# 48 matmul products of the last pair on plain 32-bit floats, half of them split into two column halves

## The chip, the cores and the metric

The kernel runs on one core of a Trainium2 chip. The metric is the device time of one execution in microseconds; smaller is better. The core has five engines that work side by side, each on its own queue of instructions: TensorE (PE, the matmul array of 128 by 128 cells; its weight loads are listed apart, as PEld), VectorE (DVE), ScalarE (ACT), GpSimd (POOL) and SyncE (SP), which here issues the transfers between the device's memory and the on-chip memory.

## The reference

Two parts follow each other. Windowed attention, with 8 sequences, 8 heads, 576 positions and 64 numbers a head; each position sees itself and the 63 before it:

```
scores = scale * matmul(q, k.T); scores = where(mask, scores, -1e9)
attn   = softmax(scores);        x = matmul(attn, v)        # 4608 tokens x 512
```

Then a gated feed-forward layer on the 4608 tokens, with 512 inputs, 1536 hidden numbers and 512 outputs:

```
gate = 1 / (1 + exp(-(x @ w_gate)))
val  = x @ w_val
out  = (gate * val) @ w_out
```

All of it is in 32-bit floats, and the comparison is a tight one, so a single matmul in a shorter number format does not do.

## The kernel before, in words

**Numbers.** The big products use the rounded float type of TensorE (F32R), in which one matmul is a single record. To keep the accuracy, each operand is cut into a high part and the rest (hi and lo), and a product is three matmuls: hi times hi, hi times lo of the moving side, and lo of the weights times hi. That is `three` (L583 to L587; all its matmuls have line 586 in the profile). The attention's matmuls (scores L220, transposes L301, outputs L331) are on plain floats (F32), unsplit. The scores use quarters of the array (64 rows by 64 columns), the outputs column halves (128 rows by 64 columns), and neighbouring calls lie on different parts.

**Tiles.** The 4608 tokens are 12 tiles of 384 tokens (`TT`). Tiles 0 and 1 go through the feed-forward layer in the plain way (L353 to L415). Tiles 2 to 11 go in five pairs s = 1 to 5 (`NS` is 6, so the last is `NS - 1`). For a pair the matrix product is done by a scheme of Strassen's kind: 7 products of half-sized blocks in place of 8, listed in `PRODUCTS` (L422) as weight block, input block and the one of three accumulators (`b` = 0, 1, 2) that it goes to. A later product adds to what stands in its accumulator.

**The up stage of a pair.** It runs over `NK` = 6 blocks k of the hidden dimension, in each over the 7 products n, and in each over m = 0, 1 (gate and value). One `product(s, k, n, m)` (L613) is two calls of `three`, for the two halves c of the 256 input rows: 6 matmuls. So each n has 12 matmuls, each k has 84, and the stage has 504. Every matmul has 128 by 128 weights and 384 moving columns, and its result goes to 384 of the 512 columns of an accumulator bank. After each product `combine` (L589) reads the accumulator on ACT or DVE, makes the sums of the scheme, the sigmoid (L371) and the product of gate and value (L629).

**The down stage of a pair.** `last_product` (L678) calls the same `three`, 252 matmuls. The last pair has the last up stage and the last down stage, with no attention work among them.

**Order.** Every piece of work is put in a list with a due time and a rank (`put`, L708), the list is sorted, and the pieces are emitted in that order; a planner then orders each engine's queue, but the matmuls keep the written order (`pe`, L85). The weights of product n and block k come from memory by `w_load` (L433), issued on SP's queue, into one of 7 buffers (`WB`), which a load can take when PE has used what was in it.

Of the kernel before, what the change touches and what calls it, by code (L numbers as in the profile page):

```python
# [9 lines left out]
F32 = mybir.dt.float32  # L10
# [8 lines left out]
P = 128  # L19
BLK = 64  # L20
TT = 384
# [5 lines left out]
def attn_ffn(ctx: ExitStack, tc: tile.TileContext, qT, kT, vN, w_gate, w_val, w_out, out, outT):  # L27
# [3 lines left out]
    nc = tc.nc  # L31
# [9 lines left out]
    NS = NT // 2  # L41
# [37 lines left out]
    def psum(s, i, nm):  # L79
        return ps_b.tile([P, DM], F32, name=nm, tag=f"b{s % 2}{i}")  # L80
# [4 lines left out]
    def pe(ins):  # L85
        return tc.keep_in_program_order(ins)
# [79 lines left out]
    xs, xf = {}, {}  # L166
    ld, vts, st, kk, sc_of, sums_of = {}, {}, {}, {}, {}, {}
# [200 lines left out]
    def gate_table(t, j, c):  # L368
        g = mp.tile([P, TT], F32, name=f"g_{t}_{j}", tag="g", bufs=4)
        with table_order():  # L370
            act = nc.scalar.activation(g, c, AF.Sigmoid)  # L371
        chain.append(act.ins)
        marks["gate"] = act.ins
        gates[(t, j)] = g
# [53 lines left out]
    wt, wot = {}, {}  # L428
# [114 lines left out]
    def rhs_of(eng, src, nm):  # L543


        b11, b12, b21, b22, t1 = src
        if nm == "T2" and not any(src is x for x in t2_made):
            eng.tensor_sub(out=b11, in0=b22, in1=t1)
        elif nm == "T4":
            eng.tensor_sub(out=b11, in0=b21, in1=b11)  # L550
        return {"B11": b11, "T2": b11, "T4": b11, "T1": t1, "T3": b12, "B21": b21, "B22": b22}[nm]

    t2_made = []
    GUARD = (8, 13)

    def h_early(s, k):
# [23 lines left out]
        x2, src = xs[(s, n, c)]  # L580
        nc.vector.tensor_sub(out=x2[:, 1, :], in0=src, in1=x2[:, 0, :].bitcast(F32))

    def three(ps, w2, q, x2, first, last, check=True):  # L583
        whi, wlo = (w2[:, e, q * P:(q + 1) * P] for e in range(2))
        for i, (l, r) in enumerate(((whi, x2[:, 0, :]), (whi, x2[:, 1, :]), (wlo, x2[:, 0, :]))):
            pe(nc.tensor.matmul(ps, l, r, start=first and i == 0, stop=last and i == 2,  # L586
                                skip_group_check=not check))  # L587

    def combine(st, n, nm, emit):  # L589


        ps = st[PRODUCTS[n][2]][:, :TT]

        def plus(a, tag, bufs):
            o = mp.tile([P, TT], F32, name=f"{tag}{n}_{nm}", tag=tag, bufs=bufs)
            marks["plus"] = nc.vector.tensor_add(out=o, in0=ps, in1=a).ins  # L596
            return o

        if n == 0:
            st["p1"] = mp.tile([P, TT], F32, name=f"p1_{nm}", tag="p1", bufs=2)  # L600
            nc.scalar.copy(st["p1"], ps)
        elif n == 1:
            st["u2"] = plus(st["p1"], "u", 2)
        elif n == 3:
            emit(1, 1, st[2][:, :TT], plus(st["p1"], "c", CB))
        elif n == 4:
            emit(0, 0, ps, None)
        elif n == 5:
            emit(1, 0, ps, st["p1"])
        elif n == 6:  # L610
            emit(0, 1, ps, st["u2"])

    def product(s, k, n, m):  # L613
        st, b = acc[m], PRODUCTS[n][2]
        if n < 3:
            st[b] = psum(1 + m, b, f"pr{b}_{m}_{s}_{k}")
        for c in range(2):
            three(st[b][:, :TT], wt[(s, k, m, n)], c, xs[(s, n, c)][0], n < 3 and c == 0, c == 1, n < 3)

        def emit(r, b, in0, in1):  # L620
            t, j = 2 * s + b, k + r * NK
            c = in0
            if in1 is not None:
                c = mp.tile([P, TT], F32, name=f"c{n}_{m}_{s}_{k}", tag="c", bufs=CB)
                nc.vector.tensor_add(out=c, in0=in0, in1=in1)  # L625
            if m == 0:
                gate_table(t, j, c)
            else:
                nc.vector.tensor_mul(out=hidden(s, k)[2 * r + b], in0=c, in1=gates.pop((t, j)))  # L629

        combine(st, n, f"{m}_{s}_{k}", emit)

    def hidden(s, k):

        if (s, k) not in ht:
            nm = f"{s}_{k}"

            def one(tag, bufs, i):
                return mp.tile([P, TT], F32, name=f"h{i}_{nm}", tag=tag, bufs=bufs)

            def two(pool, tag, bufs, i):
                h2 = pool.tile([P, 2, TT], F32, name=f"h{i}_{nm}", tag=tag, bufs=bufs)
                return [h2[:, 0, :], h2[:, 1, :]]

            if k < 2:
                h5 = wts.tile([P, 5, TT], F32, name=f"h_{nm}", tag=f"wp_{k}")
                t = [h5[:, i, :] for i in range(5)]
            elif k == 2:
                t = [one("hh", 3, i) for i in range(3)] + [one("hl", 3, i) for i in range(3, 5)]
            else:  # L650
                t = two(mp, "raw", RAW, 0) + two(mp, "raw", RAW, 1)
                if k == 3:
                    t.append(one("hl", 3, 2))
                else:
                    if k == 4:
                        ht[(s, "last")] = two(wts, f"wo_{WOB}", 1, 2)
                    t.append(ht[(s, "last")][k - 4])
            ht[(s, k)] = t
        return ht[(s, k)]
# [5 lines left out]
    def h_split(nm, i, src):  # L665
        i %= EXTRA + 2 * NPR
        h2 = xp.tile([P, 2, TT], F32R, name=f"h_{nm}", tag=f"e{i}" if i < EXTRA else f"x{i - EXTRA}")
        nc.scalar.copy(h2[:, 0, :], src)  # L668
        nc.vector.tensor_sub(out=h2[:, 1, :], in0=src, in1=h2[:, 0, :].bitcast(F32))  # L669
        return h2  # L670

    def h_part(s, n, k):
        i = n * NK + k
        with tc.issue_after(marks["plus"]) if GUARD[0] <= i < GUARD[1] else nullcontext():
            hs[(s, n, k)] = h_split(f"{n}_{s}_{k}", i, rhs_of(nc.vector, hidden(s, k), PRODUCTS[n][1]))


    def last_product(s, n, k, qs=(0, 1)):  # L678
        b = PRODUCTS[n][2]
        for q in qs:  # L680
            st = acc[q]
            if n < 3 and k == 0:
                st[b] = psum(1 + q, b, f"y{b}_{q}_{s}")
            three(st[b][:, :TT], wot[(s, n, k)], q, hs[(s, n, k)], n < 3 and k == 0, k == NK - 1, n < 3)
            if k == NK - 1:
                combine(st, n, f"y{q}_{s}", lambda r, bb, in0, in1, q=q: emit_out(s, n, q, r, bb, in0, in1))
# [90 lines left out]
    for i in range(KINDS * NF):  # L777
        j, m = divmod(i, KINDS)
# [39 lines left out]
    for s in range(1, NS):  # L818
# [15 lines left out]
        for k in range(NK):  # L834
            if s == 1:
                for m in range(2):
                    make = (-28 + 7 * m, -29 + 6 * m)[k] if k < 2 else -25 + 8 * m
                    put(now + make - 6, 7, sums_load, m, k)
                    put(now + make, 7, sums_make, m, k)
                    for i, at_cut in zip((0, 2), (-14 + 2 * m, -10 + 2 * m) if k == 0 else (-13 + 1.5 * m, -5 + 1.5 * m)):  # L840
                        put(now + at_cut, 7, sums_split, m, k, i)
                        put(now + at_cut + 4, 7, sums_store, m, k, i)
                for n, d in ((0, -23 if k == 0 else -14), (4, -12 if k == 0 else -2), (5, -9 if k == 0 else -1)):
                    put(now + d, 7.5, w_load, s, k, n)
            else:
                for n in range(NPR):
                    put(now - 22 + 2.1 * n, 7.5, w_load, s, k, n)
            for n in range(NPR):
                for m in range(2):
                    put(now, 9, product, s, k, n, m)  # L850
                    now += PRT
                    if m == 0:
                        attend(("u", NPR * k + n - 0.5))
                attend(("u", NPR * k + n))
            put(now + 0.5, 5, h_prep, s, k)
            if k < EXTRA:
                put(now + 3, 5.1, h_early, s, k)
# [23 lines left out]
        for i, tm in enumerate(at_down):  # L881
            if i < EXTRA + 2 * NPR:
                when = max(t0 - 14.5 + 2.1 * ((i - EXTRA) // 2 + 1), t0 - 5.2 if GUARD[0] <= i < GUARD[1] else t0 - 15, {5: t0 + 0.8, 11: t0 + 0.9, 17: t0 + 1}.get(i, t0 - 20))
            else:
# [19 lines left out]
    for tm, _, f, a in events:  # L904
        if f in (conv_a, conv_b, conv_c):
            with ExitStack() as behind:
# [4 lines left out]
                j, m = divmod(a[0], KINDS)  # L911
# [56 lines left out]
```

## Time and profile before

| | |
|---|---|
| median of 2 runs | 961.32 us (961.26 to 961.37) |
| the profiled execution's own time | 961.67 us |
| its span, first to last instruction | 959.9 us |
| mean granted TensorE clock | 0.998 |
| matmul records in all | 7164 |
| of them on line 586, up products | 2520 |
| of them on line 586, down products | 1260 |

The profile is of one execution. A row of a group reads: line, engine, operation, output tile <- input tiles, array rows and columns used, partitions by elements, type, count, then busy time and mean duration. Both float types of TensorE are shown as f32. Matmuls are pipelined, and a recorded duration holds the way through the array; the time from one start to the next says how many fit in a stretch. "Idle before" is what an engine waited just ahead of the group.

### The profile page before, as it was taken

Reading aid. Unit: us, or ns where it says so; the run is one execution under the profiler, and the core shown is the slowest. Engines: PE = TensorE matmul, PEld = TensorE weight load, DVE = VectorE, ACT = ScalarE, POOL = GpSimd, SP = SyncE. Lnnn points to the kernel's source line nnn. Section 1 sums busy time; section 2 is a strip of 40 time slices with the busy share of each in tenths; the row PEclk is TensorE's granted clock in tenths of the full one; section 3 lists DMA queues with packets and bytes.
Section 4 is the critical chain, followed back from the end, with each engine's and each line's share of the span. In section 5 each row is a group of like instructions: output and inputs, shape, how many; then the busy total and the mean of one; then the engine's idle time right before and its main releaser. Section 6 shows DMA issues by size and latency. Waiting matters only on the chain.

```text
span 959.9 us, 20420 instructions
## 1 busy us (share of the span) xinstructions
PE 941.3 (98%) x7164; PEld 898.0 (94%) x7164; DVE 714.3 (74%) x1919; ACT 602.7 (63%) x1487; POOL 147.5 (15%) x232
## 2 busy tenths in 40 slices
PE   6899999999999999999999999999999999999998
PEld 5799998879998999999999999999999999999998
DVE  7898989788778985666976576796566697567782
ACT  7878878667677754766755666764666675222350
POOL 4210103703765000110100111100110100000000
PEclk9999999999999999999999999999999999999999
DMA  9899988979988999888889888879988868988464
GB/s 339 304 357 370 347 303 271 347 275 358 369 301 271 402 325 309 277 265 269 251 260 316 267 273 261 270 256 284 302 273 249 268 220 257 314 249 251 143 217 157
DMA packets 105510, 273.45 MB, mean 285 GB/s; under 512 B 11456, under 2 KB 33600, under 8 KB 105408
## 3 DMA queue, kind: packets, MB, share of 16 engines
q1 hardware_dynamic: 105408, 272.15, 84.7%
q8 instruction: 57, 0.93, 0.4%
q14 instruction: 45, 0.37, 0.1%
HBM read 220.20 MB, written 51.90 MB: 283 GB/s over the span
## 4 chain that ended last, share of the span: by engine, by line
PE 77%; ACT 6%; DVE 5%; DMA 5%; issue 3%; POOL 2%; SPq 0%; DVEq 0%; ACTq 0%; POOLq 0%
PE pr L586 42%; PE y L586 23%; PE s L220 3%; PE pp L301 2%; PE ph L362 2%; PE y L409 2%; DMA w32d<-w 2%; PE s L331 2%; ACT p L252 2%; DMA a<-w32d 1%; PE oo L331 1%; DVE w L130 1%; POOL ws L528 1%; ACT L252 1%; ACT raw L118 1%
## 5 line engine op out<-in xcount | busy, mean ns | idle before, releaser
L586 PE MATMUL pr<-x_T,wt 128*128 128x384 f32 x1224 | 227.5, 338 | 0.0
L586 PE MATMUL y<-h,wot 128*128 128x384 f32 x1260 | 219.9, 334 | 0.0
L586 PEld LDWEIGHTS y<-h,wot 128*128 128x128 f32 x1260 | 218.2, 188 | 0.6 <-DVE h L629 0.3
L586 PEld LDWEIGHTS pr<-x_T,wt 128*128 128x128 f32 x1224 | 211.6, 188 | 4.5 <-issue 3.6
L586 PE MATMUL pr<-x_B,wt 128*128 128x384 f32 x1008 | 189.4, 336 | 0.0
L586 PEld LDWEIGHTS pr<-x_B,wt 128*128 128x128 f32 x1008 | 174.7, 188 | 0.8 <-issue 0.5
L668 ACT CAST h<-h 128x384 fp32r<-128x384 f32 x210 | 102.7, 515 | 80.6 <-PE y L586 43.3
L269 POOL TENSOR_TENSOR p<-p,rs 128x384 f32<-128x384 f32 x76 | 66.4, 890 | 551.8 <-DVE rs L260 496.7
L669 DVE TENSOR_TENSOR h<-h,h 128x384 fp32r<-128x384 f32 x210 | 110.7, 554 | 26.8 <-ACT h L668 26.1
L252 ACT ACTIVATE p<-p,mn 128x128 f32<-128x128 f32 x288 | 110.9, 393 | 10.2 <-DVE mn L244 9.7
L362 PE MATMUL ph<-x,w 128*128 128x384 f32 x576 | 107.0, 339 | 1.3 <-ACT g L371 0.8
L362 PEld LDWEIGHTS ph<-x,w 128*128 128x128 f32 x576 | 99.5, 188 | 4.3 <-ACT g L371 1.4
L371 ACT ACTIVATE g<-c 128x384 f32<-128x384 f32 x90 | 46.6, 524 | 66.3 <-DVE c L625 65.9
L244 DVE CUSTOM_DVE_ANT_0 p<-s,m 128x128 f32<-128x128 f32 x288 | 65.3, 284 | 27.6 <-PE s L220 27.5
L629 DVE TENSOR_TENSOR h<-c,g 128x384 f32<-128x384 f32 x90 | 55.5, 616 | 30.2 <-ACT g L371 24.7
L371 ACT ACT_TABLE_LOAD x40 | 51.3, 1283 | 12.7 <-DVE c L625 11.4
L220 PE MATMUL s<-k,q 64*64 64x128 f32 x1152 | 46.5, 293 | 7.2 <-DMA k<-in_kT_dram 5.8
L596 DVE TENSOR_TENSOR c<-pr,p 128x384 f32<-128x384 f32 x60 | 33.0, 550 | 23.7 <-PE pr L586 23.7
L252 ACT ACT_TABLE_LOAD x39 | 50.0, 1283 | 0.7
L252 ACT ACTIVATION_READ_ACCUMULATOR p<-p,mn 128x1 f32 x264 | 49.8, 188 | 0.0
L220 PEld LDWEIGHTS s<-k,q 64*64 64x64 f32 x1152 | 34.2, 141 | 13.9 <-DMA q<-in_qT_dram 5.2
L301 PE MATMUL pp<-ident,p 128*128 128x128 f32 x288 | 42.6, 281 | 4.6 <-POOL p L269 2.6
(106 smaller groups left out, 1215.9 us busy)
## 6 DMA issues: line engine op xcount, KB each, us to landing
wt<-wd SPq DMA_DIRECT2D x186, 512.0 KB, 4.5
wot<-wod SPq DMA_DIRECT2D x105, 512.0 KB, 4.7
v<-in_vN_dram SPq DMA_DIRECT2D x48, 384.0 KB, 5.4
wd<-ws SPq DMA_DIRECT2D x48, 256.0 KB, 4.4
k<-in_kT_dram SPq DMA_DIRECT2D x48, 224.0 KB, 5.2
q<-in_qT_dram SPq DMA_DIRECT2D x48, 192.0 KB, 5.1
w32d<-w SPq DMA_DIRECT2D x36, 256.0 KB, 4.6
wd<-w SPq DMA_DIRECT2D x36, 256.0 KB, 5.8
```

The costliest lines, as they stand in the source:

```text
L220: pe(nc.tensor.matmul(sc[h][half * BLK:(half + 1) * BLK, u, :], qt[h * BLK:(h + 1) * BLK, U * BLK:(U + 1) * BLK], kt[h * BLK:(h + 1) * BLK ...
L244: nc.vector.tensor_tensor_reduce(out=pt[:, u, :], in0=sc[:, u, :], in1=masks[key], op0=ALU.add, op1=ALU.min, scale=-SCALE, scalar=3.0e38, ...
L252: exp = nc.scalar.activation(pt[:, u, :], pt[:, u, :], AF.Exp, bias=mn[:, u:u + 1], scale=-1.0, **sums)
L269: eng.tensor_mul(out=pt, in0=pt, in1=rs.unsqueeze(2).broadcast_to([P, UP, P]))
L301: pe(nc.tensor.transpose(pp[:, u, :], pt[:, u, :], ident))
L362: pe(nc.tensor.matmul(ph, l, r, start=i == 0, stop=i == len(prs) - 1))
L371: act = nc.scalar.activation(g, c, AF.Sigmoid)
L586: pe(nc.tensor.matmul(ps, l, r, start=first and i == 0, stop=last and i == 2, skip_group_check=not check))
L596: marks["plus"] = nc.vector.tensor_add(out=o, in0=ps, in1=a).ins
L629: nc.vector.tensor_mul(out=hidden(s, k)[2 * r + b], in0=c, in1=gates.pop((t, j)))
L668: nc.scalar.copy(h2[:, 0, :], src)
L669: nc.vector.tensor_sub(out=h2[:, 1, :], in0=src, in1=h2[:, 0, :].bitcast(F32))
```

## The change

In the last pair, for k = 1 only, products n = 0 to 3 are no longer done on the rounded type. The same three matmuls (hi by hi, hi by lo, lo by hi) read the same tiles as plain floats. The list `WIDE` gives for each n how many weight columns a matmul takes: 128 (n = 0 and 2: the whole array, one call as before), 64 (n = 1 and 3: two calls, for columns 0 to 63 and 64 to 127, each writing its own 64 partitions of the accumulator, with the same moving operand), or None (n = 4 to 6: unchanged). Over m, c and the three parts these are 4 x 12 = 48 products: 24 stay whole, 24 become two half calls. Data, buffers, transfers and all work on the other engines are as before.

```diff
+    WIDE = (P, BLK, P, BLK, None, None, None)
...
-    def three(ps, w2, q, x2, first, last, check=True):
+    def three(ps, w2, q, x2, first, last, check=True, cols=None):
         whi, wlo = (w2[:, e, q * P:(q + 1) * P] for e in range(2))
+        if cols:
+            for i, (l, r) in enumerate(((whi, x2[:, 0, :]), (whi, x2[:, 1, :]), (wlo, x2[:, 0, :]))):
+                for a in range(0, P, cols):
+                    pe(nc.tensor.matmul(ps[a:a + cols], l.bitcast(F32)[:, a:a + cols], r.bitcast(F32),
+                                        start=first and i == 0, stop=last and i == 2, skip_group_check=not check))
+            return
         for i, (l, r) in enumerate(((whi, x2[:, 0, :]), (whi, x2[:, 1, :]), (wlo, x2[:, 0, :]))):
             pe(nc.tensor.matmul(ps, l, r, start=first and i == 0, stop=last and i == 2,
                                 skip_group_check=not check))
...
         for c in range(2):
-            three(st[b][:, :TT], wt[(s, k, m, n)], c, xs[(s, n, c)][0], n < 3 and c == 0, c == 1, n < 3)
+            three(st[b][:, :TT], wt[(s, k, m, n)], c, xs[(s, n, c)][0], n < 3 and c == 0, c == 1, n < 3,
+                  WIDE[n] if (s, k) == (NS - 1, 1) else None)
```

## The prediction

> **What bounds the kernel now.** I read the page of the profile first, for the engine that fills the span. The columns are busy time, share of the span and number of records.
>
> ```profile
> span 959.9 us, 20420 instructions
> PE 941.3 (98%) x7164; PEld 898.0 (94%) x7164; DVE 714.3 (74%) x1919; ACT 602.7 (63%) x1487; POOL 147.5 (15%) x232
> ```
>
> PE is busy 98% of the span. A mean over the span does not say that PE is the limit where the change sits, so the next view is the chain of waits, followed back from the last instruction and printed in order of time (start, length, what). The last three PE pieces are the down products of pair 4, the up products of pair 5 (the last pair) and its down products.
>
> ```profile
> 779.83 0.35 PE pr L586 x2
> 780.18 0.85 PE oo L331 x24
> 781.03 43.88 PE y L586 x252
> 824.91 87.36 PE pr L586 x504
> 912.27 43.96 PE y L586 x252
> 956.23 0.04 DVEq L696
> ```
>
> From 824.91 the chain is 504 up products without a break, one every 87.36 / 504 = 173.3 ns. They are six k of 84 each, so the step of the change, k = 1 of the last pair, lies from about 839.5 to 854.0. The view by stretches gives busy time and count of each engine there, and at its end the granted clock, the DMA share and the rate.
>
> ```profile
> 839.50:854.00 14.50, 14.50 (x85) 14.50 (x85) 9.64 (x18) 3.47 (x8) 0.00 (x0) 1.00 0.81 252
> ```
>
> In these 14.50 us PE has no idle time at all, at full granted clock. DVE works 9.64 us and ACT 3.47. Every nanosecond added to PE here is added to the end, and there is no idle PE time here that could absorb it.
>
> **The change part by part.** Of the seven products n of this k, n = 0 and 2 (12 calls each, 24 in all) become matmuls on plain floats over the full array, and n = 1 and 3 (24 calls) become two calls each, one for every 64 columns of weights. n = 4 to 6 stay. So 48 records at 173.3 ns go away, and what replaces them must be priced from plain-float work elsewhere in the trace. Three lines have it: the scores (L220), the transposes (L301) and the attention outputs (L331).
>
> How many records is a call? The groups of the page count them.
>
> ```profile
> L301 PE MATMUL pp<-ident,p 128*128 128x128 f32 x288 | 42.6, 281 | 4.6 <-POOL p L269 2.6
> L220 PE MATMUL s<-k,q 64*64 64x128 f32 x1152 | 46.5, 293 | 7.2 <-DMA k<-in_kT_dram 5.8
> ```
>
> There are 48 head pairs (12 tiles by 4). The scores make 12 calls for each, 576 in all, and have 1152 records: a plain-float matmul is two records. A transpose (6 calls for each, 288) is one, and so are the 504 rounded-float products above.
>
> How long is a record? Here are the same three groups in stretches at full clock, from the timeline (start, length from first start to last end), and their durations (minimum, median, maximum in ns).
>
> ```profile
> 765.94 0.89 PE L220 MATMUL s<-k,q 64*64 64x128 f32 x24
> 774.16 0.81 PE L301 MATMUL pp<-ident,p 128*128 128x128 f32 x6
> 780.12 0.92 PE L331 MATMUL oo<-pT,v 128*64 128x64 f32 x24
> ```
> ```profile
> L301 PE MATMUL pp<-ident,p x6: 270/272/273, 774.2 to 774.7; 128*128 128x128 f32 x6
> L331 PE MATMUL oo<-pT,v x24: 222/222/270, 780.1 to 780.8; 128*64 128x64 f32 x24
> L220 PE MATMUL s<-k,q x24: 269/269/320, 765.9 to 766.6; 64*64 64x128 f32 x24
> ```
>
> Six transposes of 128 moving columns: (0.81 - 0.272) / 5 = 107.6 ns from one to the next, or 0.84 ns a column. The rounded-float product takes 173.3 / 384 = 0.45 ns a column at most. So a plain-float record passes its moving columns about twice. The transposes could be paced by something else, so I take a second reading that does not go by pace: a stretch in which the clock was granted at half.
>
> ```profile
> 29.20:32.40 3.20, 2.93 (x46) 2.54 (x46) 3.14 (x19) 2.26 (x11) 1.65 (x2) 0.50 1.04 408
> ```
> ```profile
> L331 PE MATMUL oo<-pT,v x24: 314/314/367, 30.9 to 32.2; 128*64 128x64 f32 x24
> L220 PE MATMUL s<-k,q x22: 417/417/471, 29.5 to 30.6; 64*64 64x128 f32 x22
> ```
>
> Halving the clock adds to a record once the full-clock time of its clocked part: 314 - 222 = 92 ns with 64 columns, 417 - 269 = 148 ns with 128. The difference, 56 ns for 64 columns, is 0.88 ns a column, again two passes. Both readings agree, so a plain-float call is two records of two passes.
>
> *Full array, 24 calls.* A record of 384 columns at the transposes' rate: 3 x 107.6 = 323 ns; two make 646 ns, 472 more than 173.3, and 24 x 472 = 11.3 us. The other end is two records each as dear as two whole rounded products, 4 x 173.3 = 693 ns (24 x 520 = 12.5 us). I take the first: it is the row with the same type and the same full array. Nothing below it is possible by a gain elsewhere, since PE has no wait here to lose.
>
> *Column halves, 24 calls of two.* L331 is this pattern: 128 rows by 64 columns, neighbouring calls on opposite halves. Its 24 records begin within 0.92 - 0.222 = 0.70 us. One after the other, two passes of 64 columns at 0.84 / 2 ns each, they would need 23 x 53.8 = 1.24 us; so the halves run side by side, in 12 pairs. Taking out the first fill (270 - 222 = 48 ns), a pair comes every (0.698 - 0.048) / 11 = 59 ns. The 320 further columns of the new pairs add 320 x 0.84 = 269: 328 ns a pair, 656 a product, 483 more than now, 24 x 483 = 11.6 us. Bounds: 646 ns as in the full array (11.3 us), and L331's pair with the fill, 63.5 ns, simply six times, 381 ns or 762 a product (14.1 us). I take 11.6, the end nearest to a row of the same form: only what goes with columns can grow sixfold.
>
> *Going in and out of the halves.* n = 1 and n = 3 are one excursion each. The chain above shows one at 780: 0.85 us where 12 pairs need 0.71, so 0.14 too much. Coming back, the first rounded product can take longer, by this row of its line:
>
> ```profile
> L586 PE MATMUL pr<-x_T,wt x1224: 331/334/446, 228.0 to 909.9; 128*128 128x384 f32 x175
> ```
>
> 446 - 334 = 112 ns, and the whole stage behind the excursion took 43.88 us against 252 x 0.1733 = 43.68, which caps the return at 0.20. So 0.25 to 0.34 us an excursion; two make 0.5 to 0.7, and I take 0.6. The Trainium skill states in "TensorEngine Tiling (Array Packing)", Key Properties, that changing the tiling mode drains TensorE; at 780 the trace agrees, with the 0.14 us. With a drain of 334 - 173 = 161 ns and an opening of 112 ns at each of the four changes the sum would get 1.1 us in place of 0.6.
>
> *The weight loads.* Their number goes from one to two or four a product. Now they cost nothing, since they run beside the matmuls:
>
> ```profile
> L586 PEld LDWEIGHTS pr<-x_T,wt x48: 187/188/188, 841.2 to 851.4; 128*128 128x128 f32 x48
> ```
>
> A load takes 188 ns by its record while products follow each other every 173.3 ns, so loads lie under matmuls and even under each other. The new cover is 323 ns a record in place of 173. Without any cover, a load costs what an opening record shows: 112 ns for 128 columns, 48 for 64. Against this stands a rule in the Trainium skill, "TensorE: Matmul & The Clock Gate", Part 3 (The mechanism): a load overlaps matmuls in flight only when the row group differs, which both column halves, on all 128 rows, never do. By it the sum would be that of the third rival below; the row speaks against it, because the full-array loads already share all rows with the matmul in flight and are hidden.
>
> *Other engines.* The change moves no instruction, adds no wait and issues no DMA. DVE and ACT get 38 us for the work they now do in 14.50. The queue behind is SP's with the weight loads from memory: seven buffers, each freed when PE has used it, so a load has six n ahead, at least 6 x 12 x 0.1733 = 12.5 us, and it lands in 4.5:
>
> ```profile
> wt<-wd SPq DMA_DIRECT2D x186, 512.0 KB, 4.5
> ```
>
> Nothing is late next; what hangs on k = 1 is late by PE's own delay.
>
> **Sum.** 11.3 + 11.6 + 0.6 = 23.5 us. The profiled execution took 961.67 us (span 959.9 and 1.8 around it), the median of the runs is 961.32, 0.35 less. So 985.2 against the profiled run, and 984.8, rounded 985, against the median. Low end: 11.3 + 11.3 + 0.5 = 23.1, or 984.4. High end: 12.5 + 14.1 + 0.7 = 27.3, or 988.6.
>
> **The rivals.**
> First, a plain-float record passes once, not twice. For it: the transposes are a special matmul, and in L301, L331 and L220 alike the number of moving columns goes with the size of the loads, so their pace might be that of loads. Then a product is 2 x 173.3 ns, the extra 48 x 173.3 = 8.3 us, with the excursions 8.9: 970, or 0.9% over now. This is the case on the other side, not slower by what a measurement can tell. It decides if a 384-column record takes under 280 ns: 2% is 19.2 us, (19.2 - 0.6) / 48 = 388 ns extra a product, 561 in all. Against it stand the 0.88 ns a column of the half clock, which is no pace.
>
> Second, the halves do not run side by side with 384 columns and a shared moving operand. Then four records of 323 ns replace one product: 24 x (1292 - 173.3) = 26.8 us, with the full array and the excursions 38.7: 1000. Against it stand the 0.70 us of L331 and the 0.89 us of L220, whose 24 records of 107.6 ns would need 2.5 us in a row.
>
> Third, the new loads lie open: 48 full ones at 112 ns and 96 halves at 48, 5.4 + 4.6 = 10.0 us on top, 995; with halves loaded side by side 993. Against it: the 188 ns above, and L331's 59 ns a pair, which leaves no room beside two passes of 64 columns.
>
> **How the numbers follow.** Forecast 0.84, single pass 0.06, halves in turn 0.05, open loads 0.04, and 0.01 for a gain through a changed order on the other engines that nothing here shows. The predicted time is that of the first. The range is its own bounds, 984.4 to 988.6, with about 1.4 us on each side for what the sum leaves out, the 0.35 between profiled run and median and small stalls: 983 to 990. The rivals, 0.16 together, stay outside. About 2% is what a measurement of this kernel can tell from no change: above 980.5 us lie the forecast, the halves in turn and the open loads, 0.92 with rounding; within 2% the single pass, 0.07 with rounding; faster 0.01.
>
> **What the profile afterwards would show.** The PE records go from 7164 to 7260 (48 go, 48 + 96 come). Line 586 gets its new form of 128 x 64 with 96 records, starting in pairs some ns apart, pairs some 328 ns apart; the full ones 323 ns apart, each recorded as about 272 + 256 x 0.84 = 487 ns. The last up stage goes from 87.36 us to about 111, still without a PE wait, and the stages around it stay. A stage near 96 us means single passes; 126 halves in turn; 121 open loads. The prediction is wrong if PE waits for another engine in that stage, or if time appears outside it.

## The result and the profile after

The changed kernel takes 984.93 us (median of two runs, 984.35 and 985.51) against 961.32 before, a ratio of 1.0246 with a 95% interval of 1.0202 to 1.029: slower, by 23.6 us. The forecast was 985.0. The profiled execution took 984.35 us, 22.7 more than the one before.

The page of the changed kernel, span and engines:

```profile
span 982.6 us, 20612 instructions
PE 962.3 (98%) x7260; PEld 902.8 (92%) x7260; DVE 714.8 (73%) x1919; ACT 603.7 (61%) x1487; POOL 147.8 (15%) x232
```

PE has 7260 records, the 96 more that were worked out, and 21.0 us more busy time; the rest of the 22.7 is idle time of PE in the part ahead, where the first 780 us hold 763.42 us of PE work in place of 765.08. The busy times of DVE, ACT and POOL are the same within 1 us. The chain of waits in order of time (start, length, what) says where the time came in; line 589 is the new matmul, line 593 the old one, which was 586:

```profile
780.39 43.88 PE y L593 x252
824.27 14.56 PE pr L593 x84
838.83 31.46 PE pr L589 x144
870.29 64.68 PE pr L593 x372
934.97 43.95 PE y L593 x252
```

The last up stage lasts 14.56 + 31.46 + 64.68 = 110.70 us where it had 87.36: 23.34 more, as much as the whole kernel grew, within what the runs scatter. The down stages before and behind it are as they were (43.88 and 43.88, 43.95 and 43.96). The stage is again one unbroken piece of PE work, as the view by stretches shows for the 31.5 us of plain floats (busy time and count of PE, PEld, DVE, ACT, POOL; clock; DMA share and rate):

```profile
838.80:870.30 31.50, 31.50 (x146) 15.52 (x144) 4.93 (x9) 1.76 (x4) 0.00 (x0) 1.00 0.24 80
```

DVE, ACT and the DMA engines are far from busy here, at full clock on PE; their work on these four products is spread out, since the 48 calls had 48 x 0.1733 = 8.3 us before and have 31.5 now. The rows of the new line (duration minimum, median, maximum in ns, first and last start):

```profile
L589 PEld LDWEIGHTS pr<-x_T,wt x120: 133/137/190, 846.5 to 869.5; 128*64 128x64 f32 x96, 128*128 128x128 f32 x24
L589 PE MATMUL pr<-x_T,wt x120: 486/486/590, 846.5 to 869.8; 128*64 128x384 f32 x96, 128*128 128x384 f32 x24
L589 PE MATMUL pr<-x_B,wt x24: 485/486/486, 838.7 to 846.1; 128*128 128x384 f32 x24
```

24 whole-array records begin within 846.1 - 838.7 = 7.4 us: 23 steps of 322 ns, each record 486 ns long. The 96 half records have the same 486 ns.

The profile of before and those of the runs below begin this last part anywhere from 779.7 to 782.9 us, with the same work ahead of it; the times of the kernel before range from 959.1 to 964.7. So the lengths of the stage, which repeat to some hundredths, are compared in what follows, and the times only say that nothing else moved.

### The profile page after: what moved, and what is told of

Read it like the earlier page. It is cut to its first block, busy times and chain, and to the rows that moved or that the text cites. A ratio compares the mean times of both kernels' runs of the same rounds, so it can differ in the third digit from the quotient of the medians.

```text
span 982.6 us, 20612 instructions
## 1 busy us (share of the span) xinstructions
PE 962.3 (98%) x7260; PEld 902.8 (92%) x7260; DVE 714.8 (73%) x1919; ACT 603.7 (61%) x1487; POOL 147.8 (15%) x232
## 4 chain that ended last, share of the span: by engine, by line
PE 85%; DMA 5%; ACT 3%; DVE 3%; issue 2%; POOL 1%; SPq 0%; DVEq 0%; POOLq 0%
PE pr L593 42%; PE y L593 22%; PE ph L362 6%; PE y L409 3%; PE pr L589 3%; PE s L220 3%; PE pp L301 2%; PE s L331 2%; DMA w32d<-w 1%; ACT p L252 1%; PE oo L331 1%; DMA raw<-in_moe_w_val_dram 1%; DMA v<-in_vN_dram 1%; PE pr L331 1%; DMA wt<-wd 1%
## 5 line engine op out<-in xcount | busy, mean ns | idle before, releaser
L593 PE MATMUL pr<-x_T,wt 128*128 128x384 f32 x1188 | 221.1, 338 | 0.0
L593 PEld LDWEIGHTS pr<-x_T,wt 128*128 128x128 f32 x1188 | 205.3, 188 | 4.5 <-issue 4.0
L593 PE MATMUL pr<-x_B,wt 128*128 128x384 f32 x996 | 187.3, 336 | 0.0
L593 PEld LDWEIGHTS pr<-x_B,wt 128*128 128x128 f32 x996 | 172.6, 188 | 1.2 <-issue 1.1
L220 PE MATMUL s<-k,q 64*64 64x128 f32 x1152 | 45.1, 287 | 7.3 <-DMA k<-in_kT_dram 5.2
L608 ACT COPY p<-pr 128x384 f32<-128x384 f32 x60 | 26.9, 475 | 33.6 <-PE pr L593 26.5
L306 ACT COPY pT<-pp 128x384 f32<-128x384 f32 x96 | 41.4, 481 | 9.3 <-PE pp L301 9.1
```

The costliest lines, as they stand in the source:

```text
L220: pe(nc.tensor.matmul(sc[h][half * BLK:(half + 1) * BLK, u, :], qt[h * BLK:(h + 1) * BLK, U * BLK:(U + 1) * BLK], kt[h * BLK:(h + 1) * BLK ...
L306: cp = nc.scalar.copy(pT, pp)
```

## The experiments

**The 24 whole products alone.**

```diff
-    WIDE = (P, BLK, P, BLK, None, None, None)
+    WIDE = (P, None, P, None, None, None, None)
```

> Only n = 0 and 2 on plain floats, whole array; n = 1 and 3 as before. Theory (two records of two passes a product, 322.5 ns each as the changed kernel's trace has them, nothing for a change of type): the up stage of the last pair goes from 87.36 us to 87.36 + 24 x (645 - 173.3) = 98.7 us, the whole to about 972.6. Rival (the whole-array products are cheaper than the halves and most of the 23.3 us comes from the halves): clearly under 96 us. Rival (a change of type costs something like a change of tile): over 99 us.

The time was 973.77 us, a ratio of 1.0123 (1.0094 to 1.0152). The chain:

```profile
826.15 14.56 PE pr L593 x84
840.71 7.74 PE pr L589 x24
848.45 2.08 PE pr L593 x12
850.53 7.74 PE pr L589 x24
858.27 66.56 PE pr L593 x384
```

24 records in 7.74 us are 322.5 ns each, 645 a product; the stage is 98.68 us. The 12 rounded products in between still take 2.08 us, 173.3 ns each: going from one float type to the other and back costs nothing on the whole array.

**The 24 products in halves alone.**

```diff
-    WIDE = (P, BLK, P, BLK, None, None, None)
+    WIDE = (None, BLK, None, BLK, None, None, None)
```

> Only n = 1 and 3 on plain floats in column halves; n = 0 and 2 as before. Theory (halves side by side at 322.5 ns a pair, and 0.35 us for each of the two excursions into the halves): up stage 87.36 + 11.3 + 0.7 = 99.4 us, the whole about 973.3. Rival (halves one after the other): 87.36 + 26.8 + 0.7 = 114.9 us. Rival (excursions cost nothing): 98.7 us.

973.38 us, a ratio of 1.0122 (1.0091 to 1.0152). The chain:

```profile
823.61 16.64 PE pr L593 x96
840.25 7.89 PE pr L589 x48
848.14 2.30 PE pr L593 x12
850.45 7.89 PE pr L589 x48
858.34 64.70 PE pr L593 x372
```

48 half records, 24 pairs, last 7.89 us, 0.15 more than 24 whole records. The rounded stretch behind each is 0.2 longer (2.30 for 2.08; 64.70 for 372 x 0.1733 = 64.47). So a pair costs what one whole record costs, and an excursion 0.15 + 0.2 = 0.35 us. The stage is 99.42 us.

**All 48 whole.**

```diff
-    WIDE = (P, BLK, P, BLK, None, None, None)
+    WIDE = (P, P, P, P, None, None, None)
```

> All 48 products on plain floats over the whole array, no halves. Theory: 87.36 + 48 x (645 - 173.3) = 110.0 us for the up stage, 0.7 less than the changed kernel, the whole about 984.0. Rival (the halves save time, because two small loads are cheaper than a large one or two streams share a pass): over 110.7 us. Rival (halves cost more than their excursions): under 109.5 us.

985.05 us, a ratio of 1.0241 (1.0207 to 1.0274). The chain:

```profile
825.02 14.56 PE pr L593 x84
839.58 30.96 PE pr L589 x96
870.54 64.48 PE pr L593 x372
```

96 records in 30.96 us, 322.5 each, and 110.00 us for the stage: 0.70 less than with halves, which no comparison of whole times shows (985.05 and 984.93). The halves neither save nor cost anything but their two excursions.

**Whole and halves in turn, call by call.**

```diff
+    turns = [1]
...
             for i, (l, r) in enumerate(((whi, x2[:, 0, :]), (whi, x2[:, 1, :]), (wlo, x2[:, 0, :]))):
+                turns[0] += 1
+                cols = (P, BLK)[turns[0] % 2]
                 for a in range(0, P, cols):
```

> The same 48 products, 24 whole and 24 in halves, but in turn, call by call: 24 excursions into the halves in place of two. Theory (each excursion costs 0.35 us, as the changed kernel's trace has it: 0.09 before the first pair, 0.05 in it, 0.09 before the next whole product and 0.11 in it): up stage 110.0 + 24 x 0.35 = 118.4 us, the whole about 992.7. Rival (the cost comes with the change of type at the ends, or is hidden between plain-float neighbours): 110.0 to 111 us.

993.98 us, 1.0342 (1.0298 to 1.0386). In the chain of this kernel line 592 is the plain-float matmul, 596 the other:

```profile
826.42 14.56 PE pr L596 x84
840.98 39.12 PE pr L592 x144
880.10 64.68 PE pr L596 x372
```

The stage is 118.36 us, where 118.4 was expected: (118.36 - 110.00) / 24 = 0.35 us an excursion. It is the change between whole array and halves that costs, not the type, and the price adds up one by one.

**The halves one after the other.** The instructions are the same as in the changed kernel, in another order.

```diff
-            for i, (l, r) in enumerate(((whi, x2[:, 0, :]), (whi, x2[:, 1, :]), (wlo, x2[:, 0, :]))):
-                for a in range(0, P, cols):
+            for a in range(0, P, cols):
+                for i, (l, r) in enumerate(((whi, x2[:, 0, :]), (whi, x2[:, 1, :]), (wlo, x2[:, 0, :]))):
```

> The changed kernel with the two loops of the half calls exchanged: the three matmuls of columns 0 to 63 first, then the three of 64 to 127. The same instructions, but neighbouring calls now lie on the same half. Theory (halves overlap only with a neighbour on the other half, in the order of the queue): 8 triples, each 12 records of 322.5 ns in a row in place of 6 pairs, so 15.5 us on top of 110.7 us, less at most one record of overlap at each of the some 14 borders between halves (4.5 us): up stage 121.7 to 126.2 us, the whole 996 to 1000. Rival (PE finds the partner further back in its queue, or splits differently): 110.7 us as in the changed kernel.

986.11 us, 1.025 (1.0207 to 1.0294). The chain, and the row of line 589 in the first 0.72 us of an excursion:

```profile
825.11 14.56 PE pr L593 x84
839.67 32.85 PE pr L589 x144
872.52 64.70 PE pr L593 x372
```
```profile
L589 PE MATMUL pr<-x_T,wt x2: 486/512/537, 847.3 to 847.7; 128*64 128x384 f32 x2
```

The stage is 112.11 us: only 1.41 more than with neighbours on opposite halves, not the 11 to 15.5 of my theory, which falls here. The row shows why there is a delay at all: in 0.72 us only the first half has begun its records. The record that opens a half is known by its 537 ns, and the second half opens at 848.04, 0.70 us late, just after the third record of the first half; from there both halves work every 322.5 ns, one ahead of the other, and at the end of the excursion the second has the same 0.70 us left. Two excursions make the 1.4.

**Twelve records in a row on each half.** If a half takes records ahead into a queue of its own, one at work and three waiting (with six in a row, the seventh could go out when the third began), then a longer run must block it.

```diff
-    def three(ps, w2, q, x2, first, last, check=True, cols=None):
+    def three(ps, w2, q, x2, first, last, check=True, cols=None, at=None):
...
-                for a in range(0, P, cols):
+                for a in range(0, P, cols) if at is None else (at,):
...
-        for c in range(2):
-            three(st[b][:, :TT], wt[(s, k, m, n)], c, xs[(s, n, c)][0], n < 3 and c == 0, c == 1, n < 3,
-                  WIDE[n] if (s, k) == (NS - 1, 1) else None)
+        wide = WIDE[n] if (s, k) == (NS - 1, 1) else None
+        for at in (0, BLK) if wide == BLK else (None,):
+            for c in range(2):
+                three(st[b][:, :TT], wt[(s, k, m, n)], c, xs[(s, n, c)][0], n < 3 and c == 0, c == 1, n < 3, wide, at)
```

> The changed kernel with all six calls of a product on columns 0 to 63 first, then all six on 64 to 127: twelve records in a row on one half, where the run with exchanged loops had six. In that run the second half began when the third of the first half's six records began, and from then on both halves worked without a break. Theory (each half has a short queue of its own, one record at work and three waiting, and the common queue stops when the next record's half is full): the second half starts when the ninth of twelve begins, 8 records after the first, and so on in turn; an excursion of four runs lasts 36 records in place of 24, 2 x 12 x 0.3225 = 7.7 us more than in the changed kernel, up stage 118.4 us (two waiting: 120.4). Rival (PE looks ahead without such a limit): 110.7 to 112.5 us. Rival (only direct neighbours overlap): 126 us.

992.43 us, 1.0326 (1.0282 to 1.037). The chain, then line 589 in the first 2.60 us of an excursion and in the next 1.30:

```profile
824.05 14.56 PE pr L593 x84
838.61 39.53 PE pr L589 x144
878.14 64.71 PE pr L593 x372
```
```profile
L589 PE MATMUL pr<-x_T,wt x8: 486/486/537, 846.3 to 848.6; 128*64 128x384 f32 x8
L589 PE MATMUL pr<-x_T,wt x9: 486/486/537, 848.6 to 849.9; 128*64 128x384 f32 x9
```

118.80 us against 118.4 expected, 8.1 more than the changed kernel. Eight records begin alone in the first 2.60 us; the second half's opening record (537) comes in the next stretch, at 848.92, 5 ns behind the ninth of the first half. Three are then still to come on the first half. So the halves are independent, as far as the queue of one half lets the common stream of instructions through. By these two runs alone the limit could also be a look-ahead of fixed length for the whole array; the run with quarters tells them apart.

**Quarters.**

```diff
-    WIDE = (P, BLK, P, BLK, None, None, None)
+    WIDE = (P, BLK // 2, P, BLK // 2, None, None, None)
```

> n = 1 and 3 in four calls of 32 columns in place of two of 64. Theory (every column part has its own stream, and four go side by side as two do): one set of four records every 322.5 ns, up stage 110.7 us as in the changed kernel, the whole about 985. Rival (the streams share a port of which two are the limit): 24 x 645 ns more, 126.2 us, the whole about 1000.

986.71 us, 1.0266 (1.0223 to 1.031). The chain:

```profile
826.74 14.56 PE pr L593 x84
841.30 31.43 PE pr L589 x240
872.74 64.68 PE pr L593 x372
```

110.67 us. Four column parts go side by side as two do; 192 records of 32 columns take what 96 of 64 took. No limit of shared streams was met. The first records of the four quarters begin within 20 ns, from 848.97 to 848.99. With two records a call, that of the fourth quarter is the seventh in the order of the instructions. In the run with exchanged loops the seventh record, the first of the other half, had to wait until the third began. A look-ahead of one fixed length for the whole array would have held back both, so the limit belongs to each column part.

**The loads' cover taken away.** Products n = 3 to 6, 48 as well, each matmul cut into six of 64 moving columns.

```diff
-    WIDE = (P, BLK, P, BLK, None, None, None)
+    WIDE = (None, None, None, BLK, BLK, BLK, BLK)
...
-                for a in range(0, P, cols):
-                    pe(nc.tensor.matmul(ps[a:a + cols], l.bitcast(F32)[:, a:a + cols], r.bitcast(F32),
+                for a in range(0, TT, cols):
+                    pe(nc.tensor.matmul(ps[:, a:a + cols], l.bitcast(F32), r.bitcast(F32)[:, a:a + cols],
```

> 48 products (n = 3 to 6) on plain floats over the whole array, each matmul cut into six of 64 moving columns, so six times as many weight loads for the same columns moved. It takes the loads' cover away: a record moves 64 columns twice in some 54 ns, a load of 128 columns opens at 107 ns. Theory (a load is hidden only as far as the record before it is long): 576 records of 107 ns, 61.6 us for the 48 products, up stage 79.04 + 61.6 = 140.7 us, the whole about 1015. Rival (loads of neighbours overlap each other and never set the pace): 576 x 56 = 32.3 us, stage 111.3. Rival (loads are never hidden): 576 x (107 + 54) = 92.7 us, stage 171.8.

1017.59 us, 1.0588 (1.0538 to 1.0637). The chain:

```profile
825.70 20.80 PE pr L593 x120
846.50 64.26 PE pr L589 x576
910.76 58.30 PE pr L593 x336
```

A stage of 143.36 us: 64.26 / 576 = 111.6 ns a record, for 64 columns twice, so now the load sets the pace. It is somewhat dearer than the 107 I had put in, but it still overlaps with the matmul: in a row the two would take 54 + 107 = 161.

**The same chunks in halves.** The loop also runs over the two halves, so each chunk is a pair with loads of 64 columns.

```diff
-    WIDE = (P, BLK, P, BLK, None, None, None)
+    WIDE = (None, None, None, BLK, BLK, BLK, BLK)
...
-                for a in range(0, P, cols):
-                    pe(nc.tensor.matmul(ps[a:a + cols], l.bitcast(F32)[:, a:a + cols], r.bitcast(F32),
+                for u, a in [(u, a) for u in range(0, TT, BLK) for a in range(0, P, cols)]:
+                    pe(nc.tensor.matmul(ps[a:a + cols, u:u + BLK], l.bitcast(F32)[:, a:a + cols], r.bitcast(F32)[:, u:u + BLK],
```

> As the run with chunks of 64 moving columns over the whole array (64.26 us for its 576 records, 111.6 ns each), but every chunk in two column halves: 1152 records in 576 pairs, each with a load of 64 columns. Theory (the loads of the two halves run side by side, each half with its own, so a pair is as long as two passes of 64 columns, 59 ns as in the attention outputs): 576 x 0.059 = 34.0 us, and one excursion of 0.35: up stage 79.04 + 34.3 = 113.4 us, the whole about 988. Rival (the loads of the halves follow each other, or wait for the matmul of the other half because both use all rows): 107 to 112 ns a pair, stage 140.7 to 143.5, the whole about 1017.

988.53 us, 1.0281 (1.0251 to 1.0311). The chain of this kernel:

```profile
825.24 20.80 PE pr L593 x120
846.05 13.56 PE pr L589 x458
859.61 0.48 issue
860.08 7.70 PE pr L589 x255
867.78 0.33 issue
868.11 13.05 PE pr L589 x439
881.16 58.44 PE pr L593 x336
```

From 846.05 to 881.16 are 35.11 us for 576 pairs, 0.81 of it in two stops that the profile files as issue, waiting for nothing that it shows; 13.56 us for 229 pairs are 59 ns a pair. The stage is 114.36 us against 113.4 expected, the stops being most of the difference, and their cause stays open. The same columns moved and the same weights loaded as in the run before take 29 us less, which fits each half having its own load under its own matmul.

Column halves on the rounded type were not measured, so what an excursion between rounded products alone would cost stays open.

## Why the prediction was right

**PE is the limit, with no idle time in the stage.** Held: the stage is one unbroken piece of PE work, 23.34 us longer, and the profiled execution is 22.7 us longer, the 0.6 between them lying ahead of the stage. Nothing behind it became late.

**Two records of two passes.** A record takes 322.5 ns; 323 was taken from the transposes. The rival of a single pass, with a stage near 96 us, is refuted by 110.70. Of the two readings in the trace before, the half clock was the one that could not be mistaken for the pace of loads, and the chunk run shows that the doubt was not idle: with 64 columns moved per load, the load does set the pace. At 111.6 ns that pace lies so near the transposes' 107.6 ns that the transposes alone could not have told passes from loads. The trace of before spoke more strongly against the single pass than the prediction says: moving columns and load size do not go together in L220, whose loads are of 64 columns as in L331, while it moves 128:

```profile
L220 PEld LDWEIGHTS s<-k,q x24: 129/133/134, 765.9 to 766.4; 64*64 64x64 f32 x24
L331 PEld LDWEIGHTS oo<-pT,v x24: 133/138/139, 780.1 to 780.8; 128*64 128x64 f32 x24
```

By the rows in the prediction, the 24 records of L220 are six sets of four on the quarters, some (0.89 - 0.269 - 0.051) / 5 = 114 ns apart, where the pairs of L331 are 59 ns apart: twice the moving columns, about twice the time, with loads as wide. Whether a record really passes its columns twice or takes each at half the pace, the runs do not tell apart; the time per column is what they show.

**24 whole products, 11.3 us.** Measured 98.68 - 87.36 = 11.32.

**24 products in halves, 11.6 us.** Mis-sized a little: 328 ns a pair added the transposes' 0.84 ns a column, which holds a share of their fixed part, to the 59 ns of the attention outputs, which hold a fixed part already. The 320 further columns cost 322.5 - 59 = 263.5 ns, not 269. A pair takes 322.5, no more than a whole record, so 11.32 us without the excursions.

**Excursions, 0.6 us.** Measured 0.70, the upper end of what the chain of before gave. The Trainium skill's rule in "TensorEngine Tiling (Array Packing)", Key Properties, that a change of the tiling mode drains TensorE, fits the 0.35 us that each excursion costs in the alternating run. My reading of it, 1.1 us, charged the full opening at four changes and was too high.

**Sum.** 11.3 + 11.6 + 0.6 = 23.5 against 11.32 + 11.32 + 0.70 = 23.34. The profiled run came out at 984.35, not 985.2, since the part ahead of the stage was 0.6 us shorter, which is scatter. The two misses, 0.3 us too much for the halves and 0.1 too little for the excursions, partly cancel. That 985.0 and the median of 984.93 lie so close is luck, as the two runs are 1.2 us apart; the sum itself is 0.2 us off in the stage.

**Halves in turn.** Refuted: the stage is 110.70 us, not 126. My own account of why the halves go side by side was incomplete, though, as I took it as a matter of neighbouring calls on opposite halves. The runs with six and twelve in a row showed that each half works as if from its own queue of one record at work and three waiting, and the run with quarters that this is no limit of the whole array; the order of the calls matters only when more than that lies on one half. The Trainium skill says in "TensorEngine Tiling (Array Packing)", Key Properties, that tiles operate independently and that different tiles can load weights and multiply in parallel; the trace agrees, with 59 ns a pair in the run of chunks in halves, loads and matmuls together.

**Open loads.** Refuted: the stage is 110.70 us, not 121, and 322.5 ns leave no room for 107 beside two passes. The rule in "TensorE: Matmul & The Clock Gate" of the Trainium skill, Part 3 (The mechanism), that a load overlaps matmuls in flight only when the row group differs, taken without the exception for a background weight buffer that the same section makes, does not hold here: 59 ns a pair on halves that use all 128 rows, and 111.6 ns in place of 161 on the whole array. The measurement decides.

**Confirmed signs.** 7260 records, 96 of the form 128 x 64, 486 ns each (487 expected), a stage of 110.7 us (111 expected), PE without a wait.

## What to carry to other kernels

Where one engine is busy without a gap, a change to its instructions can be priced from the same kind of instruction elsewhere in the trace, if the part that grows with the columns and the fixed part are told apart; a stretch at half clock helped with that, and the sum came within 0.2 us of the stage here. A product on plain floats took 3.7 times as long as one on the rounded type (645 for 173.3 ns), and column parts that share one moving operand gave nothing back, except where the loads would set the pace: with 64 moving columns they took 35.1 us in place of 64.3, still more than the 31.0 of uncut calls on the whole array. What they are worth where they do different work was not measured. Group the calls that leave the whole array: every excursion cost 0.35 us here.

## What the runs showed that was not expected

Each column half behaves as if it had a queue of four records, one at work and three waiting: runs of six delay one half by 0.70 us once an excursion, while runs of twelve stretch an excursion from 24 record times to some 36. So matmuls do not always start in the written order: in the run of twelve the thirteenth record began 5 ns behind the ninth. Going between float types on the whole array is free (2.08 us for 12 rounded products between two plain-float stretches). Half a plain-float record of 384 columns, 322.5 / 2 = 161 ns, is shorter than a rounded record, 173.3 ns; what the 12 ns are was not found out.
